# Layer 1 of a fast-attention and MLP kernel: chunks of 1024 tokens with 512-column matmuls in place of chunks of 512 with 256-column ones

## The chip, the cores and the metric

The kernel runs on one core of a Trainium2 chip. The metric is the device time of one execution in microseconds (us). Time before is the median of 3 runs.

## The reference

Eight batches of 8 heads, 576 tokens and 64 channels per head go through an attention with 128 random features; the heads, side by side, give 4608 tokens of 512 channels. A low-rank mixing over the tokens is added, then two layers with a ReLU between them (512 to 2048 to 512) and a residual.

```python
kv  = einsum('bhsm,bhsd->bhmd', phi(k), v);  z = sum_s phi(k)
x   = einsum('bhsm,bhmd->bhsd', phi(q), kv) / (einsum('bhsm,bhm->bhs', phi(q), z) + 1e-6)
u   = x + ((x^T @ U) @ V)^T            # mixing over the 576 tokens of a batch
out = u + relu(u @ w_ch1) @ w_ch2      # layer 1: 512 x 2048, layer 2: 2048 x 512
```

All arrays are fp32. The change concerns `relu(u @ w_ch1)`, layer 1, and what prepares its operands.

## The kernel before, in words

**Products.** Each fp32 operand is split into a high part in TensorE's fp32r format (a cast, L508 on ScalarE) and a low part, the remainder (a subtraction, L512 on VectorE or POOL). A product is then three matmuls: high by high, low by high, high by low. Both layers use the Strassen-Winograd scheme: 2 x 2 blocks, seven products (`PRODUCTS`) in place of eight, with sums of blocks ahead (S1 to S4 of the weights, T1 to T4 of the tokens) and adds of results behind. The names `uh`/`ul` are the high and low parts of the tokens' operands, `wh`/`wl` those of the weights.

**Layer 1** (`unit`, matmuls at L979). The tokens are in `NCH` = 9 chunks of `PAIR` = 512, the 2048 hidden columns in `NG` = 4 weight groups of 512. A unit is one chunk by one group: seven products, each of two halves f of the hidden columns by two halves k of the depth by three matmuls of 256 columns: 84 matmuls. The products go into four PSUM banks (`places`: a, b, d, e, a, d, e); two sets of four banks alternate between units, so that a unit has a set to itself while the unit ahead is emptied. Behind the products ScalarE copies the first (L984), VectorE does five adds (L967) that also empty the banks, ScalarE applies ReLU (L963), and the result tiles g11, g22, g21 and g12 are sent to DRAM, two transfers of 128 KB each (L957, issued on SP's queue).

**Operands of the tokens.** `prepare` brings a chunk from DRAM (`u_dram`), where the mixing left it, in 16 strided transfers (L546, in runs of 128 bytes); VectorE transposes it in four instructions (L569), POOL forms four sums (L503), then come seven casts (L508) and seven subtractions (L512). This is done for the next chunk while the present one is multiplied.

**Weights** come in a packed form that VectorE, ScalarE and POOL decode (`decoding`; L150, L151 and L154 on VectorE, L174 on POOL). Groups 1 and 2 (numbers 0 and 1 in the code) are decoded ahead, during the attention. Groups 3 and 4 are decoded beside the opening units of layer 1, with their sums on VectorE (L246). All four groups then stay on chip. The weights of layer 2 are decoded during layer 1, four groups again, and their parts are kept in DRAM (`w2_dram`) until they are split.

**Order of the work.** Each engine executes its instructions in the order in which this code emits them. The unit generator yields after every product, and between the products the other generators (decoding, preparation of the next chunk) are advanced by fixed counts (`chores`, `step`, `advance`). The order of units is

```python
order = [(0, 0), (0, 1), (1, 0), (1, 1), (0, 2), (1, 2), (0, 3), (1, 3)]
order += [(c, g) for c in range(2, NCH) for g in range(NG)]
```

The first two units belong to the opening: they are placed beside the last steps of the mixing (L422, L446, L455). **Layer 2** (L1357, 36 steps of 84 matmuls of 256 columns) follows; each step loads a block `graw` of layer 1's output (1 MB) and splits it (L1170, L1196, L1203).

Of the kernel before, what the change touches and what calls it, by code (L numbers as in the profile page):

```python
# [29 lines left out]
def performer_mlp_kernel(ctx: ExitStack, tc, q, k, v, omega, U, V, w1, w2, out):  # L30
# [40 lines left out]
    NCH = B * S // PAIR  # L71
    NG = NF // 4
    u_dram = [dram.tile([PAIR, DM], F32, name=f"u_dram{i}") for i in range(NCH)]
    g_dram = [[dram.tile([2, P, 4, 4, P], F32, name=f"g{i}_{j}") for j in range(2)] for i in range(NCH)]
# [5 lines left out]
    wpools = {g: wa for g in range(EARLY_GROUPS)}  # L80
# [3 lines left out]
    idle = const.tile([P, P], F32, name="idle")  # L84
# [7 lines left out]
    wk = attn.enter_context(tc.tile_pool(name="wk", bufs=2))  # L92
    omh = mp.tile([P, 2, M], F32R, name="omh")
# [9 lines left out]
    outer, roomy = {}, []  # L103

    def depth():
        return 2 * RB if roomy else RB

    def raw_place(j, base):
        n = j + base
        if roomy and n >= 0 and n // 2 % 2:  # L110
            if n // 2 not in outer:
                outer[n // 2] = roomy[0]()
            return outer[n // 2][:, n % 2]
        return dec.tile([P, PIECE, 2], U32, name="raw", bufs=RB)

    def decoding(jobs, late, lean, base, hold=(), defer=(), wide=0):
# [5 lines left out]
        def fetch(i):  # L122
            while fetched[0] < min(i, len(jobs)):
                j = fetched[0]
                raws[j] = raw_place(j, base)[:, : jobs[j][1], :]
                jobs[j][0](raws[j])
                fetched[0] += 1
# [9 lines left out]
        fetch(depth())  # L137
# [4 lines left out]
        for i, job in enumerate(jobs):  # L142
# [21 lines left out]
            for j, slot in enumerate(slots):  # L164
# [6 lines left out]
                if j == (2 if i < wide else len(slots) - 1):  # L171
                    fetch(i + 1 + depth())
# [13 lines left out]
        while rest:  # L186
            rest.pop(0)()
# [17 lines left out]
    wops, ready, held, kept = {}, set(), [], {}  # L205
    w2_pair, w2_sums = {}, {}

    spares = []

    def w_slot(g, i):  # L210
        i = (i - 2) % 7 if g == NG - 1 else i
        return [wpools[g].tile([P, 2, 2 * P], F32R, name=f"w{a}{g}_{i}") for a in "hl"]

    def operand(g, i):
        if (g, i) not in wops:
            if g == NG - 1 and i < 2:
                if not spares:
                    room = late["rx"].tile([P, 2, PIECE, 2], U32, name="graw0").bitcast(F32R)
                    spares.extend(room.rearrange("p s (k t) w -> p (s k) (t w)", k=2)[:, j] for j in range(4))
                wops[g, i] = [x.rearrange("p (k t) -> p k t", k=2) for x in spares[2 * i : 2 * i + 2]]  # L220
            else:
                wops[g, i] = w_slot(g, i)
        return wops[g, i]

    class Half:


        def __init__(self, g, half):
            self.g, self.half, self.v = g, half, {}
            self.sums, self.lows = (nc.gpsimd, nc.gpsimd) if g < EARLY_GROUPS else (nc.vector, nc.gpsimd)  # L230
# [9 lines left out]
        def sum(self, name):  # L240
            x, y, op = SUMS[name]
            if name in INPLACE:
                to = self.v[INPLACE[name]]
            else:
                to = dec.tile([P, 2 * P], F32, name="ws", bufs=4)
            self.sums.tensor_tensor(out=to, in0=self.v[x], in1=self.v[y], op=op)  # L246
# [5 lines left out]
        def low(self, i):  # L252
            h, l = (x[:, self.half, :] for x in operand(self.g, i))
            engine = nc.vector if self.g >= EARLY_GROUPS and i % 2 else self.lows
            K(engine.tensor_tensor(out=l, in0=self.v[LEFT[i]], in1=f32(h), op=ALU.subtract))
            ready.add((self.g, self.half, i))

        def after(self):
            first = [lambda n=n: self.sum(n) for n in ("S1", "S3", "S2")]
            rest = []  # L260
            for i in range(7):
                if LEFT[i] == "S4":
                    rest.append(lambda: self.sum("S4"))
                rest += [lambda i=i: self.high(i), lambda i=i: self.low(i)]
            return first, rest

    def w1_jobs(g):
        for half in range(2):
            h = Half(g, half)
            first, rest = h.after()  # L270
            if g == EARLY_GROUPS and half == 0:
                held.extend(first + rest)
                first, rest = [], []
# [1149 lines left out]
```

## Time and profile before

| | |
|---|---|
| median of 3 runs | 1071.03 us (1064.41 to 1072.37) |
| the profiled execution | 1066.09 us, of which its span 1064.2 us |
| TensorE (PE) busy | 1038.4 us, 98% of the span, granted clock 0.99 on average |
| VectorE (DVE) busy | 862.9 us, 81% |
| ScalarE (ACT) busy | 613.5 us, 58% |
| GpSimd (POOL) busy | 503.9 us, 47% |
| moved by DMA | 175.51 MB, 165 GB/s on average |
| the stretches | attention and mixing up to about 325 us, layer 1 to about 698 us, layer 2 from there |

Times in rows are microseconds unless marked ns. The page has the busy time of each engine, the span in 40 slices (each digit is a busy share in tenths; a slice is 26.6 us here), the DMA queues, the chain of work that ended last, and the costliest groups of instructions. A window row reads: from:to, length, then for each engine its busy time and number of instructions (PE, PE's weight loads, DVE, ACT, POOL), then the granted TensorE clock, the busy share of the DMA engines, and GB/s. A group row reads: line, engine, operation, output<-inputs, shapes, count, then busy time and mean ns of one, then idle time just before them and what ended most of it. A timeline row reads: start, duration, engine, line, operation, and in brackets the idle time before it and what ended it. Matmuls are pipelined, so a row's duration is longer than the distance between two starts; the distance is what a matmul costs.

### The profile page before, as it was taken

Reading aid. Unit: us, or ns where it says so; the run is one execution under the profiler, and the core shown is the slowest. Engines: PE = TensorE matmul, PEld = TensorE weight load, DVE = VectorE, ACT = ScalarE, POOL = GpSimd, SP = SyncE. Lnnn points to the kernel's source line nnn. Section 1 sums busy time; section 2 is a strip of 40 time slices with the busy share of each in tenths; the row PEclk is TensorE's granted clock in tenths of the full one; section 3 lists DMA queues with packets and bytes.
Section 4 is the critical chain, followed back from the end, with each engine's and each line's share of the span. In section 5 each row is a group of like instructions: output and inputs, shape, how many; then the busy total and the mean of one; then the engine's idle time right before and its main releaser. Section 6 shows DMA issues by size and latency. Waiting matters only on the chain. (4 is left out here: it accounts for less than half of the span.)

```text
span 1064.2 us, 23868 instructions
## 1 busy us (share of the span) xinstructions
PE 1038.4 (98%) x8497; PEld 1015.6 (95%) x8497; DVE 862.9 (81%) x1510; ACT 613.5 (58%) x1479; POOL 503.9 (47%) x453
## 2 busy tenths in 40 slices
PE   8999999999998899999999999999999999999998
PEld 7898999989987899999999999989999999999998
DVE  3798898997998866766587576779999999989995
ACT  4989889889764646435345444744344444444442
POOL 3446957777334532341234214535745445445443
PEclk8999999999999899999999999999999999999999
DMA  8688787685337665876778857964455454454451
GB/s 132 137 157 146 152 191 137 125 207 106 90 61 192 170 166 140 233 227 174 181 203 211 203 156 221 303 195 160 172 169 169 140 175 163 142 173 162 143 171 45
DMA packets 380486, 175.51 MB, mean 165 GB/s; under 512 B 275664, under 2 KB 353488, under 8 KB 375760
## 3 DMA queue, kind: packets, MB, share of 16 engines
q1 hardware_dynamic: 378000, 173.70, 62.6%
q8 instruction: 67, 1.10, 0.4%
q10 hardware_dynamic: 2368, 0.30, 0.2%
q14 instruction: 51, 0.42, 0.1%
HBM read 109.97 MB, written 63.96 MB: 163 GB/s over the span
## 5 line engine op out<-in xcount | busy, mean ns | idle before, releaser
L756 ACT ACTIVATE e<-p_p,nm 128x128 f32<-128x128 f32 x576 | 165.6, 396 | 26.9 <-DVE nm L749 21.5
L1196 ACT CAST gh<-gs 128x512 fp32r<-128x512 f32 x140 | 86.6, 621 | 152.0 <-DVE gs L1170 75.9
L1170 POOL TENSOR_TENSOR gs<-graw 128x512 f32<-128x512 f32 x70 | 105.1, 1505 | 145.1 <-DMA graw<-g 109.1
L963 ACT ACTIVATE g<-g 128x512 f32<-128x512 f32 x105 | 66.4, 632 | 165.9 <-DVE g L967 95.1
L1203 DVE TENSOR_TENSOR gl<-gs,gh 128x512 fp32r<-128x512 f32 x140 | 135.2, 974 | 15.5 <-ACT gh L1196 13.9
L622 POOL TENSOR_TENSOR xl<-xT,xh 128x384 fp32r<-128x384 f32 x96 | 97.2, 1028 | 102.2 <-ACT xh L618 90.9
L749 DVE TENSOR_REDUCE nm<-p_p 128x4 f32<-128x512 f32 x144 | 98.1, 683 | 28.5 <-PE p_p L743 13.8
L174 POOL TENSOR_TENSOR wf<-wf,low 128x512 int32<-128x512 int32 (+2 forms) x35 | 45.0, 1286 | 145.0 <-ACT g L963 123.2
L741 PE MATMUL p_p<-omh,xh 128*128 128x256 f32 x288 | 93.7, 325 | 3.5 <-ACT e L756 3.4
L1282 POOL TENSOR_TENSOR u<-u,p 128x256 f32<-128x256 f32 x72 | 74.8, 1067 | 34.0 <-DVE u L1282 31.4
L1203 DVE TENSOR_TENSOR gl<-graw,gh 128x512 fp32r<-128x512 f32 x107 | 80.9, 772 | 7.2 <-ACT gh L1196 6.3
L1196 ACT CAST gh<-graw 128x512 fp32r<-128x512 f32 x107 | 63.9, 619 | 39.8 <-PE p_p L1357 9.5
L743 PE MATMUL p_p<-omh,xl 128*128 128x256 f32 x288 | 82.1, 286 | 0.5 <-POOL xl L622 0.5
L742 PE MATMUL p_p<-oml,xh 128*128 128x256 f32 x288 | 81.9, 284 | 0.0
L1357 PE MATMUL p_p<-wh,gh 128*128 128x256 f32 x288 | 81.1, 282 | 0.0
L1357 PE MATMUL p_p<-wh,gl 128*128 128x256 f32 x288 | 81.0, 281 | 0.0
L1357 PE MATMUL p_p<-wl,gh 128*128 128x256 f32 x288 | 80.9, 281 | 0.0
L1357 PE MATMUL p_q<-wh,gl 128*128 128x256 f32 x276 | 77.8, 282 | 0.9 <-DVE gl L1203 0.8
L1357 PE MATMUL p_q<-wh,gh 128*128 128x256 f32 x276 | 77.7, 282 | 0.0
L1357 PE MATMUL p_q<-wl,gh 128*128 128x256 f32 x276 | 77.5, 281 | 0.0
L979 PE MATMUL p_n<-uh,wh 128*128 128x256 f32 x256 | 73.2, 286 | 2.7 <-DVE g L967 2.5
L699 PE MATMUL p_n<-kv,eT 128*128 128x65 f32 x512 | 72.2, 270 | 2.8 <-DVE rec L710 1.1
(267 smaller groups left out, 4017.8 us busy)
## 6 DMA issues: line engine op xcount, KB each, us to landing
graw<-g SPq DMA_DIRECT2D x36, 1024.0 KB, 5.2
g<-g SPq DMA_DIRECT2D x282, 128.0 KB, 2.3
raw<-in_moe_w_ch_dram SPq DMA_DIRECT2D x22, 512.0 KB, 4.6
u_dram<-ut SPq DMA_DIRECT2D x36, 256.0 KB, 2.5
u<-u_dram SPq DMA_DIRECT2D x36, 256.0 KB, 2.6
out_dram<-u SPq DMA_DIRECT2D x36, 256.0 KB, 2.8
kt<-in_k_dram SPq DMA_DIRECT2D x120, 72.0 KB, 2.8
qt<-in_q_dram SPq DMA_DIRECT2D x120, 72.0 KB, 2.7
```

What stands on the lines that cost most here:

```text
L622: nc.gpsimd.tensor_tensor(out=self.xl[-1], in0=self.turned, in1=f32(self.xh[-1]), op=ALU.subtract)
L741: nc.tensor.matmul(o, part.xh[g][:, ts], oh, start=True, stop=False)
L742: nc.tensor.matmul(o, part.xh[g][:, ts], ol, start=False, stop=False)
L743: nc.tensor.matmul(o, part.xl[g][:, ts], oh, start=False, stop=True)
L749: nc.vector.tensor_reduce(out=self.nm[:, :n], in_=self.pp[:, :n], axis=AX.X, op=ALU.max, negate=True)
L756: nc.scalar.activation(out=self.e[:, j, :], in_=self.pp[:, j, :], func=AF.Exp, bias=self.nm[:, j : j + 1])
L979: K(nc.tensor.matmul(p[:, f, :], x[:, k, fs], y[:, k, :], start=first, stop=(k == 1 and y is ul), skip_group_check=True,))
L1170: K(engine.tensor_tensor(out=to, in0=self.val[x], in1=self.val[y], op=op))
L1196: K(nc.scalar.copy(out=h, in_=v))
L1203: K(nc.vector.tensor_tensor(out=l, in0=v, in1=f32(h), op=ALU.subtract))
L1282: K(engine.tensor_tensor(out=out, in0=x, in1=y, op=ALU.add))
L1357: K(nc.tensor.matmul(acc[bank][:, half, :], x[:, ks], y[:, f, :], start=(now.s == 0 and k == 0 and half == 0 and x is h and y is wh), stop ...
```

## The change

The first 512 tokens stay a narrow chunk. The other 4096 make four wide chunks of 1024 tokens, whose matmuls have 512 moving columns. A wide unit has the same 84 matmuls as a narrow one, for twice the tokens. Its two halves f are two generators that advance in turn, each with a set of four banks to itself, so that both sets are in use by the same unit. The work goes in two passes: chunks 1 to 4 by groups 1 and 2, then chunks 4 to 1 by groups 3 and 4, then the narrow chunk by groups 3 and 4. Groups 3 and 4 are decoded during pass one with their sums on POOL, and their seven parts are kept in DRAM (`w1_dram`); before pass two they are brought back and split into the places of groups 1 and 2. The tokens' operands of chunks 3, 2 and 1 are prepared a second time in pass two, and those of the narrow chunk too.

```diff
+    NW = 1 + (NCH - 1) // 2
+    WIDTH = [PAIR] + [2 * PAIR] * (NW - 1)
+    w1_dram = [dram.tile([P, 7, 2, 2 * P], F32, name=f"w1_dram{i}") for i in range(NG)]
...
     class Half:
-            self.sums, self.lows = (nc.gpsimd, nc.gpsimd) if g < EARLY_GROUPS else (nc.vector, nc.gpsimd)
...
+        def keep(self, name):
+            nc.sync.dma_start(out=w1_dram[self.g][:, LEFT.index(name), self.half, :], in_=self.v[name])
...
-    def unit(c, g, right, bank, aside=None):
+    def unit(c, g, f, right, bank):
+        tiles = range(2) if f is None else (f,)
...
         def keep(name):
-            store[name] = up.tile([P, 2, HT], F32, name="g" + name, bufs=1 + (name == "11"))
+            store[name] = gp.tile([P, 2, HT], F32, name="g" + name[0], bufs=2)
...
         def send(name, blk):
             s, k = divmod(2 * g, 4)
+            if f is not None:
+                nc.sync.dma_start(
+                    out=g_dram[c][s][:, :, blk, k + f, :].rearrange("j p t -> p j t"),
+                    in_=flat(store[name]).rearrange("p (j t) -> p j t", t=P),
+                )
+                return
...
-            for f in range(2):
-                fs = slice(f * P, (f + 1) * P)
+            for n, t in enumerate(tiles):
+                fs = slice(t * P, (t + 1) * P)
+                o = p[:, t, :] if f is None else flat(p)
...
-                u2 = aside["u2"]() if aside else up.tile([P, 2, HT], F32, name="u2", bufs=1)
+                u2 = store["12"] = gp.tile([P, 2, HT], F32, name="u2", bufs=2)
...
-                add(keep("12"), e, u2)
+                add(u2, e, u2)
...
+    second = decoding(jobs + [w2_job(f) for f in range(NF)], 0, 0, range(len(jobs) + 3, len(jobs) + NF, 4))
+    order = [(c, g) for c in range(1, NW) for g in range(2)]
+    order += [(c, g) for c in reversed(range(1, NW)) for g in range(2, NG)]
+    order += [(0, g) for g in range(2, NG)]
+    for n, (c, g) in enumerate(order):
...
+        units = [unit(c, g, f, right, banks(f)) for f in range(2)] if c else [unit(c, g, None, right, banks(n - LAST))]
+        for k in range(PRODUCTS * len(units)):
+            i, f = divmod(k, len(units))
+            next(units[f])
...
+            if n % 2 == 0:
+                if not right.step():
+                    if not nxt and c and 0 <= (c + 1 if forth else c - 1) < NW:
+                        nxt = Wide(c + 1 if forth else c - 1)
...
+            if m == 1:
+                lefts[EARLY_GROUPS].step()
+                if k == 4:
+                    w1_stage(EARLY_GROUPS + 1)
+            if m == 0:
+                lefts[EARLY_GROUPS + 1].step()
```

In the changed kernel layer 1's matmuls are at L1025, the adds at L1012, ReLU at L1008, the sends of results at L996 (wide), the transposes at L577, the casts at L504, the subtractions at L508, POOL's sums of tokens at L590, and decoding on VectorE at L149, L150 and L153. `Wide` prepares a chunk: four transposes, four sums, seven casts and seven subtractions, each of 1024 columns. In layer 2 the chunks come in reverse order, and the first two blocks of layer 1's output are loaded into tiles that layer 1 has left (`uT1`, `uT0`), not into tiles that are free only after the decoding.

The order of instructions at three places. First TensorE where unit (0,1) ends and the third unit begins. Before, unit (1,0) has 256 columns and goes product by product, both halves into one bank (`wh_0_5924` and `wl_0_5925` are here token operands that sit in weight tiles):

```order
L979 MATMUL p_q<-wh_0_5924,wh_0_1674 128x256
L979 MATMUL p_q<-wh_0_5924,wl_0_1675 128x256
L979 MATMUL p_q<-wl_0_5925,wh_0_1674 128x256
...
L979 MATMUL p_q<-wh_1_5927,wh_1_1749 128x256
L979 MATMUL p_q<-wh_1_5927,wl_1_1750 128x256
```

Now the narrow unit (0,1) is followed by a wide one, the first half into `p_p`, the second into `p_q`:

```order
L1025 MATMUL p_n<-ul,wh_6_3463 128x256
L1025 MATMUL p_p<-Uh,wh_0_1671 128x512
L1025 MATMUL p_p<-Uh,wl_0_1672 128x512
L1025 MATMUL p_p<-Ul,wh_0_1671 128x512
...
L1025 MATMUL p_q<-Uh,wh_0_1671 128x512
L1025 MATMUL p_q<-Uh,wl_0_1672 128x512
L1025 MATMUL p_q<-Ul,wh_0_1671 128x512
...
L1025 MATMUL p_p<-Uh,wh_1_1746 128x512
```

Left out are the same rows for the other half of the depth (and before, for the other half f). The first wide product needs `Uh` and `Ul` of the first wide chunk.

Second, VectorE in the opening, from an add of unit (0,0) on. Before, decoding (L150, L151, L154) and sums of weights (L246) stand between the adds:

```order
L967 TENSOR_TENSOR g_5787<-p_n,u_5680 128x512
L422 TENSOR_TENSOR ut<-ph,x 128x512
L246 TENSOR_TENSOR wf<-wf 128x256
L246 TENSOR_TENSOR ws<-ws,wf 128x256
L154 SCALAR_TENSOR_TENSOR wf<-raw,wf 128x512
L150 TENSOR_SCALAR wf<-wf 128x512
L967 TENSOR_TENSOR g_5820<-p_n,u_5680 128x512
```

Now there is no decoding; the wide transposes and subtractions stand there, up to the first adds of the wide unit:

```order
L1012 TENSOR_TENSOR g_5836<-p_n,g_5836 128x512
L577 STREAM_TRANSPOSE uT_5879<-uraw 128x1024
L1012 TENSOR_TENSOR g_5893<-p_n,u_5820 128x512
L577 STREAM_TRANSPOSE uT_5879<-uraw 128x1024
L1012 TENSOR_TENSOR u_5820<-p_n,u_5820 128x512
L508 TENSOR_TENSOR Ul<-uT_5719,Uh 128x1024
L508 TENSOR_TENSOR Ul<-uraw,Uh 128x1024 x3
L1012 TENSOR_TENSOR u_5967<-p_p,g_5939 128x512
```

The decoding has moved behind the opening; the last transposes stand two instructions ahead of the subtractions whose results the wide unit needs.

Third, VectorE and SP in a wide unit of pass one. VectorE, unit (2,0):

```order
L149 TENSOR_SCALAR wf<-wf 128x512
L508 TENSOR_TENSOR Ul<-uraw,Uh 128x1024
L150 TENSOR_SCALAR wf<-wf 128x512
L508 TENSOR_TENSOR Ul<-uraw,Uh 128x1024
L1012 TENSOR_TENSOR g_6234<-p_n,u_6142 128x512
L1012 TENSOR_TENSOR g_6247<-p_kv,u_6151 128x512
L153 SCALAR_TENSOR_TENSOR wf<-raw,wf 128x512
```

SP's queue of transfers in the same place: sends of results (L996), loads of the next chunk (L541), parts of weights that are kept (L249):

```order
L996 DMA g_0_70<-u_6142 128x4x128
L249 DMA w_dram_85<-wf 128x256 x2
L996 DMA g_0_70<-u_6151 128x4x128
L249 DMA w_dram_85<-ws 128x256 x2
L541 DMA uraw<-u_dram_66 32x32x32 x11
L196 DMA raw<-in_moe_w_ch_dram 128x1024
L249 DMA w_dram_85<-wf 128x256
L996 DMA g_0_72<-g_6361 128x4x128
```

Decoding, subtractions of 1024 columns and adds stand in one queue on VectorE; on SP the copies of kept parts, which wait for POOL's sums, and the chunk's loads stand ahead of sends.

More of the change, by code (lines that the diff above doesn't have):

```diff
@@ L186, in decoding @@
         while rest:
-            rest.pop(0)()
+            for _ in range(3):
+                if rest:
+                    rest.pop(0)()
             yield
@@ L269, in w1_jobs @@
             h = Half(g, half)
[L270 to L273, printed above, removed]
-            if g == NG - 1:
-                kept[half] = rest
-                rest = [lambda h=h: ready.add((h.g, h.half))]
+            todo = list(h.after())
             for c in range(2):
@@ L1094, in performer_mlp_kernel @@
-    KEPT = 11
-    def bring(i):
-        for half, rest in kept.items():
-            while i < PRODUCTS and (NG - 1, half, i) not in ready:
-                rest.pop(0)()
-    def both(nxt):
-        raw = lambda: dec.tile([P, PIECE], I32, name="low", tag="de", bufs=2).bitcast(F32).rearrange("p (k t) -> p k t", k=2)
-        aside = {"u2": temporary, "22": temporary, "21": raw, "12": raw}
-        first = unit(0, NG - 1, early, banks(7))
-        other = unit(1, NG - 1, guest, banks(8), aside)
-        bring(0)
-        bring(1)
-        for i in range(PRODUCTS):
-            next(first)
-            nxt.step(i)
-            next(other)
-            bring(i + 2)
-            nxt.step(i)
-            nxt.step(i)
-            if i == PRODUCTS - 1:
-                for o in range(2):
-                    moved = w_slot(NG - 1, o)
-                    for to, x in zip(moved, wops[NG - 1, o]):
-                        K(nc.scalar.copy(out=to, in_=f32(x)))
-                    wops[NG - 1, o] = moved
@@ L1122, in performer_mlp_kernel, with staged @@
-    for _ in begun:
-        for _ in range(3):
-            guest.step()
-        chores(1, 0)
+    late["U"] = ctx.enter_context(tc.tile_pool(name="U", side="right", reuse_waits="tile", bufs=1))
+    late["rx"] = ctx.enter_context(tc.tile_pool(name="rx", side="right", reuse_waits="tile", bufs=1))
+    for _ in begun:
+        guest.step(-1)
+        guest.step(7)
+    def staged(g, src, tiles, place, lows):
+        parts = []
+        for i in range(7):
+            parts.append(tiles(i))
+            nc.sync.dma_start(out=parts[-1], in_=src[:, i])
+        return Given(dict(zip(RIGHT, parts)), place, lows)
@@ new lines, in w1_stage, with u_half @@
+    def w1_stage(g):
+        if g == EARLY_GROUPS:
+            room = [turned(h).rearrange("p k (a t n) -> p (k a) t n", a=2, t=2) for h in range(2)]
+            place = lambda i: room[i // 4][:, i % 4]
+        else:
+            place = lambda i: up.tile([P, 2, HT], F32, name="ul", bufs=UB)
+        lefts[g] = staged(g, w1_dram[g], place, w_place(g), (VE, G_, VE, G_, VE, G_, VE))
+    halves = []
+    def u_half(_):
+        tile = late["U"].tile([P, 2, PAIR], F32R, name=("Uh", "Ul")[len(halves) % 2], bufs=7)
+        halves.append(tile)
+        return [tile[:, j].rearrange("p (k n) -> p k n", k=2) for j in range(2)]
@@ L1333, in final @@
             nc.sync.dma_start(out=self.rows[1], in_=self.u[1])
-    NS = NCH * 4
+    NS = len(stretch)
+    for g in range(2):
+        while w2_ops[g].step():
+            pass
     post = iter(())
```

465 lines of the change are left out of this document (232 added, 233 removed).

## The prediction

> **What bounds the kernel now.** I read the page's busy shares first, then its slices, then the chain of waits.
>
> ```profile
> PE 1038.4 (98%) x8497; PEld 1015.6 (95%) x8497; DVE 862.9 (81%) x1510; ACT 613.5 (58%) x1479; POOL 503.9 (47%) x453
> ...
> PE   8999999999998899999999999999999999999998
> ...
> DVE  3798898997998866766587576779999999989995
> ...
> PE 33%; DMA 1%; issue 0%; ACT 0%; SPq 0%; DVE 0%; ACTq 0%
> ```
>
> TensorE is the bound: 98% busy, and 33 of the 35 points that the chain names are its own. VectorE is the next engine, and in the slices of layer 1 (about slices 14 to 26) it is the less loaded of the two. So three things can move the end: how long the matmuls take, how long TensorE stands, and whether VectorE stays beneath it. The windows show them:
>
> ```profile
> 338.00:376.00 38.00, 31.82 (x225) 30.74 (x224) 32.93 (x53) 20.09 (x43) 19.87 (x18) 0.87 0.73 186
> 400.00:700.00 300.00, 299.63 (x2520) 299.05 (x2519) 204.51 (x297) 152.80 (x275) 100.94 (x77) 1.00 0.75 203
> 697.86:717.86 20.00, 18.25 (x147) 17.43 (x146) 13.37 (x15) 9.27 (x18) 7.83 (x6) 1.00 0.65 211
> ```
>
> From 400 to 700 us layer 1 runs without a pause: 2520 matmuls in 299.6 us, **118.9 ns** for each 256-column one, with VectorE at 204.5/300 = 68% and POOL at 34%. Two places lose time. At 338 to 376 us, 225 matmuls at 118.9 ns are 26.8 us of 38: **11.2 us** lost. At the passage to layer 2, 147 are 17.5 us of 20: **2.5 us** lost.
>
> **The matmuls.** The product units of chunks 1 to 4 (new numbering) hold 16 units x 84 = 1344 matmuls of 512 columns in place of 2688 of 256. Layer 2 and chunk 0 keep theirs. Layer 1 had no 512-column matmul, but the opening has some, in short bursts at full clock:
>
> ```profile
> 318.41 0.40 PE L446 MATMUL py<-ml,su 128*128 128x512 f32 x1
> 318.65 0.40 PE L414 MATMUL ph<-y,sv 128*128 128x512 f32 x1
> 318.88 0.40 PE L446 MATMUL py<-mh,su 128*128 128x512 f32 x1
> 319.12 0.39 PE L446 MATMUL py<-ml,su 128*128 128x512 f32 x1
> ...
> 325.21 0.39 PE L446 MATMUL py<-mh,su 128*128 128x512 f32 x1
> 325.44 0.39 PE L446 MATMUL py<-ml,su 128*128 128x512 f32 x1
> 325.67 0.28 PE L979 MATMUL p_p<-uh,wh 128*128 128x256 f32 x1
> ```
>
> What counts is start to start: 0.23 to 0.24 us, which I take as 231 ns. Two of 256 columns cost 237.8. So the wider form saves 6.8 ns a pair: 1344 x 6.8 = **-9 us**. The ends: 236 ns gives -2; if nothing but the columns counted, with the per-matmul overhead halved outright, I would set 226 ns, -16. The weights are loaded half as often, but PEld is already hidden in the window (299.05 against 299.63), so nothing more comes of that.
>
> The Trainium skill ("TensorE: Matmul & The Clock Gate", Back-to-back issue gap) gives N/2.4 + 2.5 ns for isolated warm matmuls: 216 ns at 512 columns, and by its figure this term would be about -29 us. The same formula gives 109 ns at 256 columns, where the window shows 118.9, so I don't use it in the sum.
>
> **The opening.** The 11.2 us are two stalls, each followed by matmuls at half rate, and a smaller stall later:
>
> ```profile
> 340.54 0.28 PE L979 MATMUL p_n<-ul,wh 128*128 128x256 f32 x1
> 343.29 0.58 PE L979 MATMUL p_n<-uh,wh 128*128 128x256 f32 x1 [2.48 <-DVE g L967]
> 343.67 0.42 PE L979 MATMUL p_n<-uh,wl 128*128 128x256 f32 x1
> 343.89 0.42 PE L979 MATMUL p_n<-ul,wh 128*128 128x256 f32 x1
> ...
> 357.91 0.28 PE L979 MATMUL p_q<-wl,wh 128*128 128x256 f32 x1
> 360.96 0.58 PE L979 MATMUL p_kv<-wh,wh 128*128 128x256 f32 x1 [2.77 <-DVE g L967]
> ```
>
> Both wait for a VectorE add (L967) that frees a PSUM bank; it is late because VectorE works through decoding and sums of weight groups 3 and 4 ahead of it. After 2.5 us of idling the matmuls start 0.22 us apart, half speed. The change takes that decoding out of the opening, so both stalls should go. But the first wide unit, which stands right behind unit (0,1), needs the turned chunk 1: a transpose, a cast on ScalarE queued behind a ReLU, a subtraction on VectorE that competes with POOL's sums. I put 4.4 to 7 us of new idling there (a 1024-column transpose, cast and subtraction, 3.5 us by the durations below, plus one ReLU, plus up to one POOL sum) and 1.6 to 4.6 us of half rate (14 to 39 matmuls' worth of 118 ns lost, the extent behind the two old stalls): 6 to 11.7, I take 8.5, near the middle. Against 11.2: **-2.7 us** (-5 to +1).
>
> **VectorE in pass one.** Its rows, 400 to 700 us, then two shorter forms and the subtraction under contention:
>
> ```profile
> L967 DVE TENSOR_TENSOR g<-p_n,u 128x512 f32<-128x512 f32 x42 | 29.0, 689 | 11.7 <-PE p_n L979 7.5 <-DMA g<-g 3.0
> L512 DVE TENSOR_TENSOR ul<-uT,uh 128x512 fp32r<-128x512 f32 x28 | 24.0, 856 | 2.5 <-ACT uh L508 2.3
> L569 DVE STREAM_TRANSPOSE uT<-uraw 128x512 f32<-128x512 f32 x24 | 16.2, 692 | 0.0
> L150 DVE TENSOR_SCALAR wf<-wf 128x512 f32<-128x512 f32 x16 | 13.8, 864 | 13.4 <-ACT wf L132 13.4
> L151 DVE TENSOR_SCALAR wf<-wf 128x512 uint32<-128x512 uint32 x16 | 9.7, 608 | 0.0
> L154 DVE SCALAR_TENSOR_TENSOR wf<-raw,wf 128x512 uint32<-128x512 uint32 x8 | 5.5, 682 | 0.0
> ...
> L614 DVE STREAM_TRANSPOSE xT<-kt 128x384 f32<-128x384 f32 x48 | 27.4, 571 | 4.3 <-DMA kt<-in_k_dram 2.3 <-POOL xl L622 1.3 <-DMA qt<-in_q_dram 0.4
> L1282 DVE TENSOR_TENSOR u<-p_n,u 128x256 f32<-128x256 f32 x28 | 11.5, 413 | 2.8 <-PE p_n L1357 2.0 <-POOL u L1282 0.6
> ...
> L512 DVE TENSOR_TENSOR ul<-uT,uh x28: 677/684/1695, 404.8 to 660.8; 128x512 fp32r<-128x512 f32 x28
> ```
>
> From 384 to 512 columns a transpose grows by 121 ns, so 1024 columns cost about 0.692 + 4 x 0.121 = 1.18 us. From 256 to 512 an add grows by 276 ns, so 1024 cost 0.689 + 0.552 = 1.24 us; the subtraction alike, from its median 684, 1.24. Its mean was 1.25 times its median, so 1.24 to 1.55 under contention. For five units of pass one I count in the order of instructions 50 adds (34.5 us), 12 transposes (14.2), 16 subtractions (19.8 to 24.8) and 32 decoding operations (about 11 each of the three kinds, 23.0): **91 to 97 us**, while 420 wide matmuls last 97.0. VectorE goes from 68% to between 94 and 100% of TensorE's time. In pass two there is less decoding.
>
> That is the price of the change: the chunk preparation is made in pass one for four wide chunks and again in pass two for three of them and the narrow one, about three wide ones more than before, 12 transposes and 21 subtractions. Against it stands the bank slack: a product of both halves is 12 matmuls, 2.8 us, and a bank freed by product 2's add is needed again by product 5, 7 us after it was filled for this half (2.8 x 2.5); before, three products of 1.43 us, 4.3 us. So VectorE may run some microseconds late before TensorE stands. With the load just under 100% and 7 us of slack, I take **+4 us** over both passes. The low end is 0, the high end +9 (the 97 us figure exceeding by 3 in each of the three stretches of five units).
>
> POOL's sums also become twice as wide and stand against VectorE's subtractions:
>
> ```profile
> L503 POOL TENSOR_TENSOR ts<-uT,ts 128x512 f32<-128x512 f32 x12 | 15.6, 1304 | 2.3 <-DMA w_dram<-ts 2.0
> ```
>
> A wide one is up to 2 x 1.30 = 2.6 us. The subtraction's maximum of 1695 ns against its median of 684 shows waits of about 1.0 us, near what is left of a POOL sum; the adds out of PSUM show none in their mean. The Trainium skill ("SBUF — State Buffer", two separate sides) says that VectorE with two SBUF inputs and GpSimd lock a shared port pair for a whole instruction, so the waits would double with the sum's length; by it a subtraction that meets a sum waits up to 2.6 us, and 16 that each met half a sum would add 21 us in five units. That is above the end that I take; the trace agrees on the mechanism, but its 28 subtractions lost only 28 x 0.17 = 4.8 us with POOL 34% busy.
>
> **Buffers and queues.** The result tiles "12" and "22"/"21" now have two buffers per tag, one for each half. Product 6's tile must be added (0.69), passed through ReLU (0.63), issued and landed before the next unit's product 1 writes it:
>
> ```profile
> L963 ACT ACTIVATE g<-g 128x512 f32<-128x512 f32 x87 | 55.0, 632 | 136.1 <-DVE g L967 73.4 <-issue 45.1 <-DMA g<-g 11.6
> g<-g SPq DMA_DIRECT2D x282, 128.0 KB, 2.3
> 504.64 5.14 SPq L957 DMA_DIRECT2D g<-g  x8
> ```
>
> Eight issues took 5.14 us of SP's queue, 0.64 each. The loop is 0.69 + 0.63 + 0.64 + 2.3 to 4.6 (twice the bytes) = 4.3 to 6.6 us; there are 5.6 us until product 1's add wants the tile, and the add's own bank isn't needed for another unit. But behind that add the next bank-freeing add waits on VectorE. Where SP also issues chunk loads (up to 11 in a row in the order, 7 us at 0.64) or copies of decoded weights that wait for POOL, the loop breaks its slack. I take **+3 us**, 0 to +20 (16 units at 1.25).
>
> The transfers themselves grow too:
>
> ```profile
> DMA packets 380486, 175.51 MB, mean 165 GB/s; under 512 B 275664, under 2 KB 353488, under 8 KB 375760
> uraw<-u_dram SPq DMA_DIRECT2D x128, 64.0 KB, 2.6
> ```
>
> The three further chunk preparations read 3 x 16 x 128 KB = 6 MB, all in packets of 128 bytes, and the kept parts of two weight groups are 3.7 MB written and as much read: 14 MB on 175, most of it in layer 1, where the DMA engines are 75% busy (the second window's DMA share of 0.75). They stay under 90%, so I put no term of its own, and a late chunk load is among the causes of rival (c).
>
> **Passage to layer 2.** The chain has one wait here:
>
> ```profile
> 701.74 6.76 DMA graw<-g
> ```
>
> Layer 2's second block can now be loaded earlier, so this goes, and of the 2.5 us lost most should return. In its place the splitting of two blocks and the last weights crowd VectorE and ScalarE in the first step. I take **-1 us** (-3 to +3).
>
> **Sum.** -9 - 2.7 + 4 + 3 - 1 = -5.7; some stalls will bring half rate behind them as in the opening, and 17 matmuls that lose 0.118 us each are 2 us, so -4. The profiled execution took 1066.1 us (span 1064.2); it gives **1062**. The median of the runs is 1071.0, 5 above the profiled one, with a lowest of 1064.4: I forecast a median of **1066**.
>
> **Rivals.** (a) Cover holds: wide matmuls at 226 ns (-16), VectorE's lag stays in the slack (0), loops hold (0), opening -5, passage -3: -24, a median of 1047. For it: the slack grows from 4.3 to 7 us. Against: 231 in the rows and VectorE at 94%. By the skill's formula above it would be some 13 us less still, which the rows speak against. 25%.
> (b) The forecast, -12 to +8: 50%.
> (c) VectorE's queue becomes the bound: it executes in order, so when an add for bank A stands behind a transpose waiting for chunk loads, or behind an add waiting for a "12" tile, all later adds wait too. It decides once the lag exceeds the 5.6 to 7 us; then TensorE stalls 1.2 to 2 us in each of 16 units, half rate behind some: +19 to +32, and with the saved 9 and 2.7, +8 to +20: 1079 to 1091. 20%.
> (d) The change doesn't do what it says: sustained 512-column matmuls cost 2 x 118.9 = 238 ns, no gain; then +3 net of the opening and passage: 1074. 5%.
>
> **Chances.** A difference under 1%, 10.7 us, can't be told from none in this kernel's runs (they spread by 8). Faster: all of (a) and a tenth of (b), 0.30. Slower: two thirds of (c) and a tenth of (b), 0.18. The rest, 0.52, is within 1%. The range holds (b) whole, the near half of (a) and most of (c), and leaves out some 0.17: **1046 to 1088**.
>
> **What would show it.** Right: 1344 matmuls 230 ns apart; no stall for L1012 in the opening but one for the cast or subtraction before the first wide product; VectorE above 90% in pass one; TensorE above 97% there. Wrong: 512-column starts at 220 or at 237; stalls of a microsecond and more in every wide unit ended by VectorE, or VectorE idle on a landing; layer 2 slower than 117 to 120 ns a matmul.

## The result, and the profile after

The change makes the kernel slower: 1131.25 us median (4 runs, 1127.6 to 1136.3) against 1067.72 for the kernel before on the same chip, a ratio of 1.0596 (95% interval 1.0560 to 1.0632). The forecast was 1066, with a range of 1046 to 1088. The profiled execution took 1127.6 us, its span 1125.8, 61.6 more than before. On its page, the first lines of busy time and of the slices:

```profile
PE 1047.9 (93%) x7153; PEld 957.3 (85%) x7153; DVE 916.4 (81%) x1493; ACT 628.8 (56%) x1461; POOL 559.9 (50%) x456
...
PE   8999999999988898877997988888999999999998
...
DVE  4799998988987759574786868579999899998995
...
DMA  9788787673567596989669787885553545445451
```

TensorE falls from 98% to 93%, and its dents stand in slices 12 to 28 (28 us each); before, only two slices of that stretch were under 9. VectorE is at 9 in only two of these seventeen slices, the DMA row in four: neither is full throughout. The windows put numbers to the stretches, cut at the first and last matmul of each: opening units, wide units of pass one, of pass two, the narrow chunk, and the first 20 us of layer 2.

```profile
322.86:348.04 25.18, 22.38 (x177) 21.61 (x175) 17.36 (x25) 9.05 (x15) 7.59 (x5) 1.00 0.89 202
348.04:549.11 201.07, 170.29 (x672) 134.27 (x673) 140.25 (x163) 88.49 (x139) 83.71 (x50) 0.92 0.85 201
549.11:724.28 175.17, 159.72 (x673) 127.97 (x671) 129.25 (x153) 82.19 (x133) 86.26 (x45) 0.97 0.78 199
724.28:753.25 28.97, 23.95 (x170) 22.91 (x168) 20.38 (x28) 16.28 (x31) 10.74 (x7) 0.88 0.89 281
753.25:773.25 20.00, 13.26 (x93) 11.60 (x94) 19.36 (x24) 14.02 (x27) 11.04 (x7) 1.00 0.70 216
```

A pass has 672 wide matmuls, and most of them start 232 ns apart, which makes 155.9 us without a pause:

```profile
560.31 0.40 PE L1025 MATMUL p_p<-Uh,wh 128*128 128x512 f32 x1
560.55 0.40 PE L1025 MATMUL p_p<-Uh,wl 128*128 128x512 f32 x1
560.78 0.40 PE L1025 MATMUL p_p<-Ul,wh 128*128 128x512 f32 x1
```

So pass one loses 45 us and pass two 19. The narrow chunk's 168 matmuls are 20.0 us at 118.9 ns and take 29.0, 9 lost; the first 20 us of layer 2 hold 93 matmuls in place of 168, 8.9 lost where before lost 2.5. Against that stand 8 us saved by the wide matmuls (1344 x 6 ns) and 8 us in the opening units: their window is 5.2 us longer than 168 matmuls (25.18 less 20.0), but 1.9 of it are eight 512-column matmuls of the mixing, so 3.3 are lost where the opening lost 11.2. In sum some 64 us, near the 61.6 of the span.

What TensorE and VectorE wait for between 320 and 760 us (engine, line, what it waits for: us in total, times, longest):

```profile
PE p_n L1025 <- DVE g L1012: 45.0, 14, 8.2
...
DVE g L1012 <- DMA g<-g: 49.2, 16, 10.1
DVE u L1012 <- DMA g<-u: 32.2, 14, 6.7
DVE wf L149 <- ACT wf L131: 8.5, 5, 4.2
```

TensorE waits for VectorE's add, 45 us in 14 stalls, and VectorE, far from full, waits for transfers: the sends of `g` and `u`, the result tiles 22, 21 and 12. The longest stall shows the chain. Timelines of TensorE, VectorE and SP's queue in the changed kernel:

```profile
512.73 0.40 PE L1025 MATMUL p_q<-Ul,wh 128*128 128x512 f32 x1
521.37 0.80 PE L1025 MATMUL p_n<-Uh,wh 128*128 128x512 f32 x1 [8.24 <-DVE g L1012]
521.96 0.63 PE L1025 MATMUL p_n<-Uh,wl 128*128 128x512 f32 x1
522.39 0.63 PE L1025 MATMUL p_n<-Ul,wh 128*128 128x512 f32 x1
...
506.02 0.69 DVE L1012 TENSOR_TENSOR u<-p_n,u 128x512 f32<-128x512 f32 x1
...
517.20 0.69 DVE L1012 TENSOR_TENSOR u<-p_p,g 128x512 f32<-128x512 f32 x1 [6.70 <-DMA g<-u]
...
508.03 1.81 SPq L541 DMA_DIRECT2D uraw<-u_dram  x3
509.94 0.81 SPq L996 DMA_DIRECT2D g<-g  x1
510.80 3.54 SPq L541 DMA_DIRECT2D uraw<-u_dram  x3
514.44 0.54 SPq L996 DMA_DIRECT2D g<-u  x1
```

The add of product 6 ends at 506.7, its ReLU at 507.4; the send is issued only at 514.44, since six chunk loads and another send stand ahead of it on SP, and VectorE goes on 2.8 us after that, when it has landed. VectorE has the next unit's product 1 at the head of its queue, wanting that same tile, and waits 6.7 us; behind it stand the adds that free the banks, so TensorE stands 8.2 us and then issues matmuls 427 ns apart, near half its rate.

### The profile page after: what moved, and what is told of

It reads as the page before. It is cut to its first block, busy times and chain, and to the rows that moved or that the text cites. A ratio compares the mean times of both kernels' runs of the same rounds, so it can differ in the third digit from the quotient of the medians.

```text
span 1125.8 us, 21156 instructions
## 1 busy us (share of the span) xinstructions
PE 1047.9 (93%) x7153; PEld 957.3 (85%) x7153; DVE 916.4 (81%) x1493; ACT 628.8 (56%) x1461; POOL 559.9 (50%) x456
## 5 line engine op out<-in xcount | busy, mean ns | idle before, releaser
L661 POOL TENSOR_TENSOR xl<-xT,xh 128x384 fp32r<-128x384 f32 x96 | 97.3, 1031 | 101.3 <-ACT xh L657 83.7
L1008 ACT ACTIVATE g<-g 128x512 f32<-128x512 f32 x72 | 45.3, 633 | 165.8 <-DVE g L1012 89.8
L1209 ACT CAST uh<-gs 128x512 fp32r<-128x512 f32 x105 | 65.3, 623 | 115.9 <-DVE gs L1181 62.2
L1216 DVE TENSOR_TENSOR ul<-gs,uh 128x512 fp32r<-128x512 f32 x105 | 99.1, 951 | 14.1 <-ACT uh L1209 12.3
L1025 PE MATMUL p_n<-Uh,wh 128*128 128x512 f32 x128 | 55.8, 436 | 45.2 <-DVE g L1012 44.8
L1025 PEld LDWEIGHTS p_n<-Uh,wh 128*128 128x128 f32 x128 | 25.9, 203 | 57.0 <-DVE g L1012 50.9
L738 PEld LDWEIGHTS p_n<-kv,eT 128*128 128x128 f32 x512 | 67.7, 194 | 6.0 <-DVE eT L723 1.4
L1012 DVE TENSOR_TENSOR g<-p_n,u 128x512 f32<-128x512 f32 x38 | 26.0, 684 | 56.1 <-DMA g<-g 38.2
L692 PE MATMUL p_kv<-vt,e 128*128 128x65 f32 x480 | 67.7, 267 | 0.0
L1209 ACT CAST uh<-graw 128x512 fp32r<-128x512 f32 x79 | 47.8, 621 | 30.8 <-PE p_n L1396 8.7
L692 PEld LDWEIGHTS p_kv<-vt,e 128*128 128x128 f32 x480 | 64.6, 195 | 0.0
L780 PEld LDWEIGHTS p_p<-omh,xh 128*128 128x128 f32 x288 | 55.4, 192 | 8.6 <-ACT e L795 5.8
L718 PE MATMUL p_q<-ident,e 128*128 128x128 f32 x288 | 60.4, 279 | 0.7 <-ACT e L795 0.5
```

The costliest lines, as they stand in the source:

```text
L661: nc.gpsimd.tensor_tensor(out=self.xl[-1], in0=self.turned, in1=f32(self.xh[-1]), op=ALU.subtract)
L692: tc.keep_in_program_order(nc.tensor.matmul(o, e[:, h, :], w, start=(s == 0 and h == 0), stop=(s == NT - 1), skip_group_check=True))
L738: nc.tensor.matmul(pn[:, h, :], eT[:, h, :], kv[:, h, s // 5, :], start=True, stop=True)
L780: nc.tensor.matmul(o, part.xh[g][:, ts], oh, start=True, stop=False)
L1025: K(nc.tensor.matmul(o, x[:, k, fs], y[:, k, :], start=first, stop=(k == 1 and y is ul), skip_group_check=True,))
L1209: K(nc.scalar.copy(out=h, in_=v))
```

## The experiments

### Sends from a constant tile

```diff
-                    in_=flat(store[name]).rearrange("p (j t) -> p j t", t=P),
+                    in_=flat(store[name]).rearrange("p (j t) -> p j t", t=P) if name == "11" else ident.unsqueeze(1).to_broadcast([P, WIDTH[c] // HT, P]),
```

> The transfers of the result blocks 12, 21 and 22 of the wide units read a constant tile, not the result (same bytes, same queue, same number; the result in DRAM is not the layer's). So no add waits until a send has landed. Theory A (the two result buffers per tag come back too late, and VectorE, in order, stands at the add that waits for them) expects that the idle time of VectorE ended by a transfer (73 us at L1012 between 320 and 760 us) goes, and with it nearly all of TensorE's stalls of 60 us and the 18 us of half rate: 1060 to 1080 us. Rival B (VectorE is overloaded in pass one, as the prediction's +4 had it, only larger) expects no change, 1120 to 1131.

1131.3 us (ratio 1.0601, 1.0557 to 1.0644): the same in all, against theory A's number. But the windows split it. First row the wide units, second row 150 to 250 us, in the attention, here and then in the changed kernel:

```profile
409.05:731.21 322.16, 313.00 (x1343) 253.89 (x1344) 271.04 (x319) 172.47 (x275) 173.88 (x95) 0.99 0.73 162
150.00:250.00 100.00, 79.29 (x569) 72.69 (x569) 64.54 (x155) 63.94 (x204) 52.98 (x56) 0.86 0.92 219
```
```profile
150.00:250.00 100.00, 98.59 (x820) 94.15 (x820) 89.21 (x220) 90.16 (x294) 71.46 (x76) 1.00 0.75 154
```

Of the 128 wide sends 96, all but those of tile 11, no longer depended on any result, and they were issued far ahead of layer 1, at 92 to 291 us; they now filled the DMA engines during the attention (92% in place of 75%), which lost what layer 1 gained. The wide units took 322 us in place of 376, 10 above the 311.8 of matmuls alone. So VectorE's work, unchanged here, is not what stalls them (rival B falls for the 54 us), but this run took most of the sends' traffic out of layer 1 along with the wait, and can't part the two.

### Sends on ScalarE's queue

```diff
-                nc.sync.dma_start(
+                nc.scalar.dma_start(
                     out=g_dram[c][s][:, :, blk, k + f, :].rearrange("j p t -> p j t"),
```

> The sends of the wide units are issued on ScalarE's queue, behind the ReLU that makes the result, not on SP's, where chunk loads and kept weight parts stand ahead. Theory A1 (the send waits in SP's queue, 7 us at 507 to 514 us) expects most stalls gone: 1070 to 1090. Theory A2 (the send is issued in time but lands late, since the chunk loads fill the DMA engines: busy share 0.95 at 450 to 500 us) expects little: 1110 to 1131. Rival B: no change. ScalarE pays 96 issues of wide sends, at 0.5 us each 5 us more in 10 per unit; it has room.

1134.6 us (ratio 1.0627, 1.0584 to 1.0669), no gain. The stalls change owner, as TensorE's waits show:

```profile
PE p_p L1025 <- ACT g L1030: 20.9, 6, 5.6
PE p_n L1025 <- DVE g L1012: 18.2, 15, 3.2
```

ScalarE's copy (L1030), which empties a bank, is now late, because ScalarE stands at its own sends. ScalarE, and the transfers issued on its queue (ACTq), ahead of the end of a stall of TensorE of 5.6 us at 410.15:

```profile
401.60 0.62 ACT L1008 ACTIVATE u<-u 128x512 f32<-128x512 f32 x1
407.09 0.37 ACTq L996 DMA_DIRECT2D g<-u  x1
407.50 1.04 ACT L504 CAST Uh<-uraw 128x1024 fp32r<-128x1024 f32 x1 [5.29 <-DMA w_dram<-ws]
...
409.51 0.58 ACT L1030 COPY g<-p_p 128x512 f32<-128x512 f32 x1 [0.44 <-ACT u L1008]
```

The ReLU ends at 402.22, but the send behind it is issued only at 407.09, when another transfer has landed, and the copy stands behind it. ScalarE stood 43 us in 29 such waits. From the end of ReLU to issue a send now takes 0.4 us on average, 1.6 in the changed kernel; VectorE's waits for transfers fell, but ScalarE's took their place. So the run trades one queue that works in order for another: theory A1 gains nothing by this remedy, but it is not refuted. The Trainium skill ("DMA: Bandwidth & Descriptors", Issuing engines are not separate DMA queues) says that transfers from any engine run on the same 16 DMA engines, and that another issuer saves only issue time; this run agrees, with 3.9 us on average from issue to landing, 3.7 in the changed kernel.

### Chunk loads in long runs

```diff
-                    in_=u_dram[c][:, k : k + BLK].rearrange("(b i) j -> i b j", i=BLK),
+                    in_=u_dram[c].rearrange("(p q) j -> p (q j)", q=WIDTH[c] // PAIR)[k : k + BLK, :],
```

> The chunk loads read whole runs of 4096 bytes from DRAM (2048 for the narrow chunk), not runs of 128 bytes: same number of transfers, same bytes, other values (the tokens are mixed up, so the result is not the layer's). Theory A2 (DMA engines filled by small packets) expects 1065 to 1085. Theory A1 (the queue's order alone, with issues of 0.5 us each) expects that a good part stays, 1095 to 1120, as far as the loads' issue isn't itself held up by full DMA rings; if it is (1.2 us an issue at 508 to 514 us against 0.5), A1 and A2 are the same thing here. Rival B: no change.

1106.8 us (ratio 1.0368, 1.0315 to 1.0421): 24 us of the 64 come from the 128-byte runs, with as many transfers and bytes (the tokens come out mixed up). That lies in theory A1's range and outside A2's. The chunk loads' issues from 350 to 515 us, shortest, median and longest in ns, in the changed kernel and then here:

```profile
L541 SPq DMA_DIRECT2D uraw<-u_dram x58: 302/710/3003, 355.2 to 512.2; - x58
L541 SPq DMA_DIRECT2D uraw<-u_dram x64: 302/419/1957, 362.0 to 508.4; - x64
```

So what shortens is the time that a load's issue holds SP's queue. The wide sends wait less for their issue (0.9 us on average, 1.6 before the edit), but land no faster behind it (3.8 us, 3.7 before). The expectation allowed for this: where the loads' issues are themselves held up, the two theories are the same thing here. The Trainium skill ("DMA: Bandwidth & Descriptors", Specifications) has 512 bytes as the least for full rate; the 24 us agree that 128 is dear.

### Turned tokens kept in DRAM

```diff
-                stashes = []
+                stashes = [lambda: stash(0), lambda: stash(1)] if 0 < c < NW - 1 else []
...
-                        nxt = Wide(c + 1 if forth else c - 1)
+                        nxt = Wide(c + 1) if forth else Wide(c - 1, again=c > 1)
```

The functions for it stand unused in the changed kernel. All of chunks 3, 2 and 1 were kept, chunk 1 too, other than the expectation says.

> The turned tokens of chunks 1 to 3 are written to DRAM in pass one (two transfers of 1 MB each) and read back in pass two, in place of 16 strided loads and 4 transposes of each of chunks 2 and 3 (chunk 1 is still loaded as before where the code asks for it). Theory A (either form) expects the stalls of pass two after 600 us to shrink where a stashed chunk is prepared (6.8, 4.2, 2.1, 3.5 us and the half rate behind) and those of pass one to grow a little by the writes: 1110 to 1130. Rival B expects only VectorE's lighter load in pass two (8 transposes of 1.16 us): 1120 to 1131.

1109.7 us (ratio 1.0394, 1.0348 to 1.0440), 21.5 less, just under the range that I gave.

### More result buffers

```diff
+        ring = c > 1 or c == 1 and g < EARLY_GROUPS
...
         def keep(name):
+            if ring and name[0] == "2":
+                store[name] = late["up"].tile([P, 2, HT], F32, name="uh", bufs=UB)
...
-                u2 = store["12"] = gp.tile([P, 2, HT], F32, name="u2", bufs=2)
+                u2 = store["12"] = gp.tile([P, 2, HT], F32, name="g2" if ring and g % 2 else "u2", bufs=2)
```

> More result buffers, everything else as in the changed kernel: results 22 and 21 of the wide units of chunks 2 to 4 (and of chunk 1 in pass one) rotate through the seven narrow operand tiles that lie idle there, and the 12 tiles alternate between two tags of two. Theory A' (the loop of add, ReLU, send and landing, 5.4 us on average and 9 to 12.6 at its slowest, is longer than two buffers allow, and VectorE stands in order at the add that waits) expects the waits of L1012 for a transfer (81 us) and the stalls of 60 us to fall under 20, the stretch from the first to the last wide matmul from 376 to 320 to 335 us, and 1075 to 1095 us in all. Rival C (the chunk loads and kept parts fill the DMA engines, so lands would be late however many buffers) expects 1110 to 1131.

1095.3 us (ratio 1.0254, 1.0198 to 1.0310): 36 us less, at the upper end of theory A' and far from rival C. VectorE's waits for `g` and `u` fall from 81 to 19 us. Next in line, VectorE's first wait, then the windows of both passes:

```profile
DVE wf L149 <- ACT wf L131: 40.5, 12, 13.7
...
349.36:531.10 181.74, 166.32 (x672) 132.84 (x673) 135.27 (x163) 88.84 (x139) 86.52 (x50) 0.93 0.95 221
531.10:690.33 159.23, 154.99 (x673) 125.68 (x671) 127.51 (x153) 82.00 (x133) 85.61 (x45) 1.00 0.85 218
```

Pass two is nearly free (3.3 us lost); pass one still loses 26 us, with the DMA engines at **95%** and 221 GB/s. There VectorE waits for decoding, which waits for packed weights. ScalarE and SP's queue in this kernel:

```profile
466.42 0.66 ACT L131 ACTIVATE wf<-raw 128x512 f32<-128x512 f32 x1 [9.74 <-DMA raw<-in_moe_w_ch_dram]
...
451.98 4.55 SPq L541 DMA_DIRECT2D uraw<-u_dram  x5
456.63 0.91 SPq L249 DMA_DIRECT2D w_dram<-wf  x1
457.64 3.88 SPq L541 DMA_DIRECT2D uraw<-u_dram  x4
461.63 0.49 SPq L196 DMA_DIRECT2D raw<-in_moe_w_ch_dram  x1
```

Nine chunk loads hold the queue for 8.4 us, 0.94 each, ahead of the weights.

Only the tiles 22 and 21 (the change of `keep` alone), with `u2` as it was:

> Only the tiles of results 22 and 21 get more buffers, the 12 tiles keep two. If the tight loop is the one inside a unit (22 made by product 3 must have landed before product 5's add writes 21: 5.6 us for 0.69 + 0.63 + issue + 3.6), which I had overlooked, nearly all of the gain of the run with both comes here: within 10 us of it. If the loop from product 6 to the next unit's product 1 is the tight one, the gain is small here: over 1110.

1113.5 us (ratio 1.0413, 1.0346 to 1.0480): half of the gain, over the 1110 that was set for the loop from product 6. So both loops are too long, the one inside the unit (22 to 21) and the one from product 6 to the next product 1; the 12 tile then has the most of the waits (`u<-p_p` for `g<-u`, 45.3 us).

### Width alone undone, with more buffers

```diff
-                            o, x[:, k, fs], y[:, k, :], start=first,
+                            o[:, cols], x[:, k, fs], y[:, k, cols], start=first and q == 0,
```

> The kernel with more buffers, each 512-column matmul issued as two of 256 columns with the same weights: the width alone is undone. If TensorE is the bound again in the wide units, the time goes up by 1344 x (2 x 118.9 - 232) ns = 8 us against the kernel with more buffers; if something else bounds them, it stays the same.

1101.7 us (ratio 1.0309, 1.0255 to 1.0364): 6.4 more than the kernel with more buffers, near the 8. The two intervals overlap, so that this run alone doesn't fix the size; with the 232 ns of the rows it is as forecast.

### Buffers and stash; all tiles; the narrow chunk earlier

> The same buffers and the turned tokens kept in DRAM for pass two, as in the run with the stash. Theory A' expects little beyond the buffers alone (what is left is the opening and the passage to layer 2): 1065 to 1090. Rival C expects the stash's own gain of 22 us on top of whatever the buffers give: 1085 to 1110.

1080.2 us (ratio 1.0111, 1.0051 to 1.0171): 15 on top of the buffers' 36. The time lies in the range of A' (1065 to 1090) and under that of rival C (from 1085), but the gain is nearer to C's 22 than to the little of A'. The two edits' gains nearly add up. With tile 11 in the rotation too (`if ring:` in place of the test for names in "2"):

> The kernel with more buffers and the stash, with the tiles of result 11 in the rotation as well: in its trace TensorE still stood 9 us for ScalarE's copy into tile 11 (3.2 and 6.1 us at 420 and 466 us), a tile with two buffers like those before. If the same loop is the cause, the stretch of the wide units falls from 328 to 318 to 322 us and the time by 6 to 10: 1070 to 1075. If ScalarE is late for reasons of its own (waits for packed weights at the head of its queue, 25 us), nothing changes: 1078 to 1082.

1081.1 us (ratio 1.0102, 1.0049 to 1.0155), no gain. TensorE's waits for the copy into tile 11 fell from 9.0 to 3.1 us, but the wide units took nearly as long (327 us for 328), so other losses took their place. And with `nxt.step(7 if k > 6 else -1)` for the narrow chunk:

> As the run before this one, with the narrow chunk's operands made four half-products earlier in the last wide unit: TensorE stood 3.3 us there for a cast of ScalarE and a subtraction, with 1.3 us and more at half rate behind. Expected: 3 to 5 us less than the run before this one, about 1068, within 1% of the kernel before. If the casts then delay the last wide unit's own adds and copies, no gain.

1080.3 us (ratio 1.0092, 1.0056 to 1.0129): nothing either that these runs can tell, where 3 to 5 us were expected.

### More buffers and long runs

> The kernel with more buffers (22, 21 and 12; no stash) with chunk loads in runs of 4096 bytes, tokens mixed up. With two buffers these loads gave 24 us. Theory A' says that they shortened the loop and so act on the same loss: with more buffers the gain must be clearly smaller than 24, 5 to 15: 1080 to 1090. Rival C (the loads slow the work by themselves) expects the full 24 again: 1071.

1074.6 us (ratio 1.0041, 1.0012 to 1.0070; tokens mixed up): 20.7 less, outside what A' expected and close to rival C's 24. So the small packets do not act through the result buffers alone. The window of 350 to 515 us, here and then of the kernel with more buffers and short runs:

```profile
350.00:515.00 165.00, 160.52 (x681) 129.35 (x682) 140.41 (x164) 89.50 (x141) 88.46 (x51) 0.98 0.82 245
```
```profile
350.00:515.00 165.00, 153.72 (x629) 123.50 (x629) 123.78 (x146) 79.04 (x121) 81.26 (x46) 0.94 0.97 221
```

Short runs: DMA engines 97% busy for 221 GB/s. Long runs: 82% for 245. In the same window a chunk load's issue holds SP's queue 0.82 us on average with short runs and 0.46 with long ones, all issues together 126 and 88 of the 165 us. From issue to landing the packed weights take 5.0 us on average in either kernel. So the trace shows the small packets in the issues on SP, not in later landings; whether the full DMA engines are what holds the issues up, no run here shows.

### Packed weights from another queue

```diff
-            nc.sync.dma_start(out=raw.rearrange("p n w -> p (n w)"), in_=words(src))
+            (nc.scalar if swift else nc.sync).dma_start(out=raw.rearrange("p n w -> p (n w)"), in_=words(src))
```

`swift` holds from the first wide unit's decoding on; POOL's variant has `nc.gpsimd`.

> The kernel with more buffers (1095), and the loads of packed weights from the first wide unit on are issued on ScalarE's queue. In the trace with more buffers such a load was issued behind nine chunk loads that held SP's queue for 8.4 us (452 to 461.6 us), ScalarE waited 9.7 us for it at the head of its queue, VectorE 5.1 us for ScalarE, and TensorE stood 4.7 us. Theory D (the order in SP's queue does it) expects most of the 21 us that the loads in long runs gave: 1075 to 1085. Rival C (the DMA engines are full of small packets, so the load lands late from any queue) expects 1088 to 1097.

> The same on POOL's queue, where the load stands behind the decoding operation that frees its tile. Theory D: 1075 to 1085, if an issue on POOL costs little; rival C: 1088 to 1097. If POOL's issue itself takes microseconds, POOL's sums are late and it is slower than 1095.

> With the stash too (1080). In pass one the chunk loads are the same, so theory D expects 6 to 12 us less, 1068 to 1074, level with the kernel before; rival C 1077 to 1082.

> The same on POOL's queue: theory D 1068 to 1074, rival C 1077 to 1082, over 1082 if POOL's issue is dear.

With more buffers: 1099.5 us on ScalarE (ratio 1.0311, 1.0260 to 1.0362), 1123.8 on POOL (1.0550, 1.0484 to 1.0615), where 1095.3 was; both lie above either theory's range. With the stash too: 1081.8 (1.0142, 1.0096 to 1.0188) and 1096.7 (1.0279, 1.0225 to 1.0332), where 1080.2 was. No gain from ScalarE, so theory D, the weights' own place in SP's queue, falls; the rest of that queue stays as slow. On ScalarE's queue the DMA engines are as full:

```profile
350.00:515.00 165.00, 151.87 (x630) 121.33 (x628) 121.95 (x145) 76.06 (x119) 75.97 (x45) 0.96 0.99 228
```

On POOL an issue is not dear, but it waits its turn (idle before it, and who ended it):

```profile
L198 POOL DMA_DIRECT2D raw<-in_moe_w_ch_dram x22 | 12.4, 565 | 94.8 <-ACT Uh L506 23.1 <-issue 21.4 <-DVE wf L153 11.5
```

### Everything together

Buffers, stash and long runs in the loads that are left:

> More buffers, the stash, and the chunk loads that are left in runs of 4096 bytes (tokens mixed up). In pass one of the kernel with more buffers the DMA engines are 97% busy (350 to 515 us), and with long runs 82%. If small packets in pass one are what holds the kernel with buffers and stash (1080) back, this gives 1060 to 1070: the 20 us of the long runs less the 8 to 10 that the stash and they both give in pass two. If not, 1075 to 1080. What then remains over the saving of the wide matmuls is the opening, the last chunk's start and the first step of layer 2, some 20 us.

1071.0 us (ratio 1.0024, 0.9999 to 1.0050), just above the 1060 to 1070 for small packets; with buffers and long runs, without the stash, it was 1074.6. Both passes of this kernel:

```profile
352.36:515.21 162.85, 158.08 (x672) 127.94 (x673) 141.24 (x164) 89.86 (x142) 86.48 (x51) 0.98 0.88 267
515.21:668.80 153.59, 153.59 (x673) 126.02 (x671) 119.27 (x142) 81.93 (x132) 82.49 (x45) 1.00 0.79 241
375.48:476.76 101.28, 97.28 (x422) 78.56 (x420) 93.17 (x106) 55.12 (x87) 63.17 (x38) 1.00 0.93 286
```

The first two rows add up to 316.4 us for 311.8 of matmuls at 232 ns; the third is the second to sixth unit of pass one. That is 60 of the 64 us lost, by three edits that leave the matmuls, adds, casts and subtractions as they were. It mixes the tokens up, so it is a bound and no kernel. The fastest that compute the reference are those with buffers and stash, about 1% behind the kernel before; none here beats it.

## Why the prediction was wrong

**The matmuls: right.** Forecast 231 ns and -9 us; 232 in the rows and -8, 6.4 by undoing the width. Undisturbed, in pass two above, it is 153.59/672 = 228.6 ns. The rate of 226 ns did not come. Nor did the 216 ns by the formula of the Trainium skill ("TensorE: Matmul & The Clock Gate", Back-to-back issue gap).

**The opening: right in mechanism, the gain larger.** Both old stalls are gone, and the new one is the cast before the first wide product, 2.7 us. The opening units lose 3.3 us and the first wide product 2.6 more, with a wait for the subtraction and half rate: some 6 us, the low end of the 6 to 11.7, where 8.5 was taken.

**VectorE in pass one: the load right, the consequence priced at +4.** The forecast was 91 to 97 us of work in five units. In the changed kernel it is 98.0 in 129.4 us; that third row, over the same five units, has 93.2 in 101.3 us, with TensorE busy for 97.3. So a VectorE at 92% costs TensorE little by itself. The wide subtractions took 1.60 us on average, a little over the 1.24 to 1.55 taken:

```profile
L508 DVE TENSOR_TENSOR Ul<-uraw,Uh 128x1024 fp32r<-128x1024 f32 x21 | 30.8, 1468 | 0.0
L508 DVE TENSOR_TENSOR Ul<-uT,Uh 128x1024 fp32r<-128x1024 f32 x17 | 30.1, 1769 | 0.0
```

The 14 of these 38 with no POOL instruction beside them took 1.21 to 1.22 us, the 24 others 1.83 on average and up to 3.43.

**Buffers and queues: the step that failed.** The prediction named the loop and its slack (4.3 to 6.6 us against 5.6) and took +3, at most +20, because the add's own bank isn't needed for another unit. But what counts is what stands behind the waiting add on VectorE, which works in order; that was written down, and still priced at 1.25 us a unit at most. Three numbers were off. The loop: from the end of ReLU to landing, for which the forecast had 2.9 to 5.2 us (issue and landing), it took 5.4 us on average over the 128 wide sends, from 9.1 up for the slowest tenth, 12.6 at most, of which the wait for issue is up to 8.0. With add and ReLU that is 6.7 on average, over the 5.6 there are. A second loop was overlooked: 22 and 21 share a tag, so that 22 must land before 21 is written two products later. And most stalls bring half rate behind them, in layer 1 some 112 matmuls and 17.6 us by their starts, where 2 us stood in the sum. More buffers alone gave back 36 of the 64 us.

**The DMA engines: the other failed step.** "They stay under 90%, so I put no term of its own": in the changed kernel the share did stay there, 0.85 and 0.78 in the two passes, but the term was not nothing. The same chunk loads in long runs give 24 us, and 21 with more buffers. The load is not spread over the kernel: a wide chunk's tokens are read for two units in place of four, in packets of 128 bytes, and the kept weight parts fall into the same pass. With TensorE no longer held by the buffers the share there is 95 to 97%. The small packets were seen in longer issues on SP, which the sum took at 0.64 us each.

**Passage to layer 2: wrong sign.** -1 was forecast; 8.9 us are lost where before lost 2.5, about +6. The load wait is gone, but VectorE is busy for 19.36 of 20.00 us in the window above: the splits of two blocks and the last weights crowd it, a consequence that the prediction named and took as smaller than the gain. It stays in all the later runs, with 85 to 99 matmuls in these 20 us in place of 168.

**Rival (c)** had the mechanism, VectorE's queue behind a buffer or a load, and 20% chance. Its price of 1.2 to 2 us in each of 16 units, +8 to +20 net, was too small: the stalls are 14 of up to 8.2 us, and the whole came to +62. It stays open whether the 316 us of the wide units can be had with the tokens in the right order, since no kernel here has that without the small packets; by what way these packets slow the issues; and how much could be hidden of the 15 us that the narrow chunk and layer 2's first step lose more than before.

## What to carry to other kernels

Price a wait by what stands behind it in its engine's queue, not by the waiting instruction's own deadline. Price a loop through add, send and landing by its slow tail too, not by its mean alone, and add the half rate that most stalls brought here. A transfer that is moved to another engine's queue waits there as well, and stops that engine. When a change packs the same loads into a shorter stretch, work out the DMA engines' share for that stretch. Matmuls twice as wide double what each result loop must move per product; count the buffers again before counting the matmuls.

## What the runs showed of the hardware

In sustained streams 512-column matmuls cost 228.6 to 232 ns, two of 256 columns 237.8: the wider form saves 2 to 4%. Of the ten stalls of 2.6 to 8.2 us ahead of wide matmuls in the changed kernel, nine were followed by 6 to 11 matmuls that started 427 ns apart; one, of 3.1 us, was not. With strided loads in runs of 128 bytes the DMA engines were 97% busy at 221 GB/s, with runs of 4096 bytes 82% at 245; the issue of such a load held SP's queue 0.82 and 0.46 us on average. A 128x1024 subtraction on VectorE took 1.22 us with POOL idle and 1.83 on average with a POOL instruction beside it. Sends on ScalarE's queue stopped ScalarE for 43 us. The sends of a constant tile were issued at 92 to 291 us, far ahead of the code that names them, and their traffic moved with them.
